# Routing of the later slots in seven operations behind the leading tokens, and six row buffers

## The chip, the cores and the metric

One core of a Trainium2 chip runs the whole computation in one launch. The metric is the device time of one execution in microseconds. TensorE (PE) multiplies matrices, VectorE (DVE) and ScalarE (ACT) do the elementwise work, GpSimd (POOL) does elementwise work and issues the gathers, SyncE (SP) issues plain transfers. Each engine has a queue of its own that it works through in order; they meet at semaphores.

## The reference, cut to what matters

Three layers follow one another. Attention of 512 tokens with 32 state rows in each of 8 x 8 heads gives 4352 tokens of 512 numbers. A mixture of 8 experts sends each token to the one expert with the highest cosine, and a dense layer with a hard-swish comes behind it:

```python
expert_idx = np.argmax(logits, axis=1)            # logits = xn @ en.T / tau
for e in range(E):
    mask = expert_idx == e
    h = np.maximum(x[mask] @ w1[e], 0.0)
    out[mask] = gate_w[mask, None] * (h @ w2[e])
h = out @ w_in
return (h * np.clip(h + 3.0, 0.0, 6.0) / 6.0) @ w_out
```

Which tokens go to which expert is known only when the attention is done. All products keep single precision: each factor is split into a high part and a low part (hi and lo, wh and wl, and so on), and three products of parts are added.

## The kernel before, in words

**Stages.** The attention runs batch by batch up to about 130 us and writes the tokens with their logits to a scratch in DRAM (xd). Tokens of one expert are packed into slots of 128 rows. The expert with the most tokens is the leading expert: its first five slots (QUAD, four slots, and FIFTH, one) are known as soon as its number and each token's rank are known, and are worked on while the routing of all other slots is still computed. Then come the later units (RUN) of two slots or one, and between them the dense layer in blocks of 256 tokens (Y loads a block's tokens, F1 and F2 are its two products). The weights of the dense layer are converted along the way (`convert`); its early parts are done beside the attention and the leading slots.

**How the order is made.** Nothing is scheduled on the chip. `Sched` is a planner that runs while the program is written: each operation is given an engine or a choice of engines with a cost in microseconds (the dict, "D" for VectorE and so on), a due time (the number behind it), operations that it waits for, and places in rings of buffers that it takes and gives back. The planner plays this through and puts next what can begin first, with 0.0473 of its due time added (0.115 before the leading slots are opened). What comes out is each engine's fixed order of instructions; the real waits are those of the semaphores. An operation is not cut: all its instructions stand together in its engine's queue.

**The routing.** `o_lead` finds the leading expert and its number (L988 to L990), `o_e0` casts the number to an integer for SP (L993), `o_s0` places the leading tokens, `o_at(0)`, `o_pg(0)` and `o_gidx(0)` turn that into row numbers for the gathers. For the later slots `o_tot` (L1017 to L1043) counts each expert's slots in small tiles, `o_slot` (L1052 to L1058) gives each token its slot, in three rounds over the first, middle and last parts of an expert's slots, then `o_at(1)`, `o_pg(1)` (L1078, 34 matmuls), `o_gidx(1)`, `o_quarter` and `o_qidx` make the row numbers; `o_es` gives SP the expert of each slot, `o_cs` the row at which each slot's output goes. On VectorE `o_es` is 5.0 us by the planner's reckoning and `o_slot` 4.2.

**Queues around the change.** SP issues the loads of expert weights (`load_w`, L1244 and L1247, four raw buffers), the stores of the five leading outputs (`out_slot`, L1551) and the loads of the dense blocks' tokens (`Y`, L1586 and L1590). It reads the expert's number with a value load (L1233) ahead of the first weights. POOL issues the gathers of tokens (`X`: L1283 whole rows, L1289 quarter rows, four to a slot) and the stores of the later slots' outputs, and does part of the low weight halves (L1261). A raw weight tile is cast on ScalarE or VectorE (wh, L1258), its rest made on VectorE or POOL (wl, L1261).

**The row buffers.** One pool of 128 x 544 buffers, `row`, NROW = 5 of them, serves gathered tokens (xg and xq), tokens of a dense block (yl), the outputs before they are stored (yt, L1543 and L1547; yo) and the middle tile of a late weight conversion (cv_m). The planner's ring `row` has as many places; a second ring, `rin`, allows four of them at a time to inputs (xg, xq, yl).

**The scratch.** `dynamic_dma_scratch_size` is the part of SBUF, in bytes of each partition, that is set aside for the descriptors of POOL's transfers.

The functions that the diff touches, with the line numbers of the profile:

Of the kernel before, what the change touches and what calls it, by code (L numbers as in the profile page):

```python
# [14 lines left out]
ALU = mybir.AluOpType  # L15
AX = mybir.AxisListType
# [22 lines left out]
class Sched:  # L39
# [16 lines left out]
    def op(self, fn, cost, prio, deps=(), take=(), give=(), dma=0.0, after=None, port=""):  # L56

        o = Op()
        o.port = port
        o.fn, o.cost, o.prio, o.take, o.give, o.dma = fn, cost, prio, take, give, dma  # L60
        o.kids, o.ready, o.end, o.left = [], -99.0, None, 0
        for h in give:
            h.readers += 1
        for d, end in [(d, True) for d in deps] + [(after, False)]:
            if d is None:
                continue
            if d.end is None:
                d.kids.append((o, end))
                o.left += 1
            else:  # L70
                o.ready = max(o.ready, d.end if end else d.issued)
        if not o.left:
            self.avail.append(o)
        self.n += 1
        return o
# [79 lines left out]
def kernel(  # L155
# [13 lines left out]
    PE, ACT, DVE, POOL, SP = nc.tensor, nc.scalar, nc.vector, nc.gpsimd, nc.sync  # L169
    PSUM, DRAM = bass.MemoryType.PSUM, bass.MemoryType.DRAM  # L170
    B, H, S, D = x.shape
# [71 lines left out]
    copy = {"A": ACT.copy, "D": DVE.tensor_copy}  # L243


    NRAW, NW, NROW, NGX = 4, 3, 5, 4
    NAX, NXT, NSC, NE2, NE1, NA2, NAH, NXR = (3, 3, 1, 1, 2, 1, 1, 1)
    NHX = 4
    RG = {n: Ring(k) for n, k in dict(
# [5 lines left out]
    def hold(*names):  # L255
        return Hold(*(RG[n] for n in names))
# [642 lines left out]
    def T(shape, name, dt=F32, home=rt):  # L899
        return home.tile(shape, dt, name=name)  # L900
# [111 lines left out]
        DVE.tensor_scalar(out, out, BIG, None, op0=ALU.add)  # L1012
        DVE.tensor_scalar(out, out, -BIG, None, op0=ALU.add)

    def o_tot():

        DVE.tensor_scalar(full, cnt, 127.0 / 256, BIG, op0=ALU.add, op1=ALU.add)  # L1017
        DVE.tensor_scalar(full, full, -BIG, None, op0=ALU.add)
        DVE.tensor_scalar(lead, key, kmax[:, 0:1], float(NL), op0=ALU.is_equal, op1=ALU.mult)
        DVE.tensor_tensor(before, key.unsqueeze(1).to_broadcast([128, E, E]),  # L1020
                          key.unsqueeze(2).to_broadcast([128, E, E]), op=ALU.is_gt)

        DVE.tensor_tensor(odd, full, lead, op=ALU.subtract)
        floor_half(npair, odd)

        def prior(out, t):
            w = T([128, E, E], "prior")
            DVE.tensor_tensor(w, before, t.unsqueeze(1).to_broadcast([128, E, E]), op=ALU.mult)
            DVE.reduce_sum(out, w, axis=AX.X)

        prior(pb, npair)
        DVE.tensor_scalar(pb, pb, float(NP), 2.0, op0=ALU.min, op1=ALU.mult)
        DVE.tensor_scalar(two, pb, -1.0, 2.0 * NP, op0=ALU.mult, op1=ALU.add)
        DVE.scalar_tensor_tensor(two, npair, 2.0, two, op0=ALU.mult, op1=ALU.min)
        DVE.tensor_tensor(single, odd, two, op=ALU.subtract)
        prior(sb, single)
        DVE.tensor_scalar(pb, pb, float(NL), None, op0=ALU.add)
        DVE.tensor_scalar(sb, sb, float(NL + 2 * NP), None, op0=ALU.add)

        DVE.tensor_tensor(lo_, pb, lead, op=ALU.subtract)  # L1040
        DVE.tensor_tensor(mid_, two, lead, op=ALU.add)
        DVE.tensor_tensor(hi_, sb, mid_, op=ALU.subtract)
        DVE.tensor_tensor(hi_, hi_, lo_, op=ALU.subtract)  # L1043

    ofs = [T([128, NTILE], f"ofs{i}") for i in range(3)]

    def o_slot():
        for i, v in enumerate((lo_, mid_, hi_)):
            for c, (j0, j1) in enumerate(PART):
                n = j1 - j0  # L1050
                t = tmp[c][:, :, 0:n]
                DVE.tensor_tensor(t, hot[c][:, :, 1:n + 1], v.unsqueeze(2).to_broadcast([128, E, n]), op=ALU.mult)  # L1052
                DVE.reduce_sum(ofs[i][:, j0:j1], t.rearrange("p e j -> p j e"), axis=AX.X)
        DVE.tensor_scalar(loc, loc, -BIG, None, op0=ALU.add)
        DVE.tensor_tensor(ofs[1], loc, ofs[1], op=ALU.is_ge)
        DVE.tensor_tensor(ofs[1], ofs[1], ofs[2], op=ALU.mult)
        DVE.tensor_tensor(ofs[0], ofs[0], ofs[1], op=ALU.add)
        DVE.tensor_tensor(s16[1], loc, ofs[0], op=ALU.add)  # L1058
# [4 lines left out]
    def o_at(i):  # L1063

        n = SLOTS[i]
        t = V["at", i] = T([128, 4 if i else 3, n, NTILE], f"at{i}", BF16)
        eq = t[:, 2]
        DVE.tensor_tensor(eq, s16[i].unsqueeze(1).to_broadcast([128, n, NTILE]), iota_sj[:, 0:n], op=ALU.is_equal)
        DVE.tensor_scalar(t[:, 0], eq, pf[:, 0:1], None, op0=ALU.mult)
        for k, v in ((1, iota_j), (3, obf[:, 0]), (2, obf[:, 1]))[:3 if i else 1]:  # L1070
            DVE.tensor_tensor(t[:, k], eq, v.unsqueeze(1).to_broadcast([128, n, NTILE]), op=ALU.mult)

    def o_pg(i):
        n, k = SLOTS[i], 4 if i else 2
        p = pool["g_ps"].tile([128, 512], F32, tag="g", name="pg_g") if i else ps("pg_ps")[:, 0, :]
        p = V["pg", i] = p[:, 0:k * n].rearrange("p (a s) -> p a s", a=k)
        for j in range(NTILE):
            PE.matmul(p, V["bt", j], V["at", i][:, 0:k, :, j], start=j == 0, stop=j == NTILE - 1)  # L1078
# [80 lines left out]
        seq_ = [b_]  # L1159
    pr = t_end - 30  # L1160
    s0_op = op(o_s0, {"D": 0.35}, pr - 1, [lead_e, *loc_])
    e0_op = op(o_e0, {"D": 0.1}, pr + 3, [lead_e])
    gidx_op = []
    for i, n in enumerate(SLOTS):
        if i:
            pr = 107.5892 + 27.0094
            tot = op(o_tot, {"D": 3.4}, pr, [lead_e, cnt_op, switched])
            slot = op(o_slot, {"D": 4.2}, pr, [tot, s0_op])
        hpg = hold("gps" if i else "ps")
        a = op(lambda i=i: o_at(i), {"D": 3.9 if i else 0.7}, pr - 1, [slot if i else s0_op])  # L1170
        b = op(lambda i=i: o_pg(i), {"T": 2.3 if i else 1.3}, pr - 1, [a, *bt_], [hpg])
        gidx_op.append(op(lambda i=i: o_gidx(i), {"D": 0.6 if i else 0.35}, pr - 2, [b], (), [hpg]))
    hpg = hold("gps")
    a = op(o_quarter, {"T": 0.3}, pr, [gidx_op[1]], [hpg])
    qidx_op = op(o_qidx, {"D": 0.7}, pr, [a], (), [hpg])
    es_op = op(o_es, {"D": 5.0}, pr, [tot])
    cs_op = op(o_cs, {"D": 1.9}, pr + 10, [es_op])
    first.append(gidx_op[0])
    first.extend([lead_e, cnt_op, s0_op, e0_op, *bt_])
    lead_ops.extend([qidx_op, cs_op])  # L1180

# [573 lines left out]

    for u in (QUAD, *RUN):  # L1760
        for w in "ab":
            for i in range(4):
                load_w(u.w, w, i, [w_at[u, w, 2 * i + j] for j in range(2)])

    for u in (QUAD, FIFTH):
        for i in range(u.n):
            X(u, i, x_at[u, i])
    for k in range(8):
        for hf in range(2):
            L1w(QUAD, k, w_at[QUAD, "a", k] + 1.28 * hf, hf)  # L1770
# [113 lines left out]
```

## Time and profile before

Three runs took 1407.59, 1408.51 and 1410.87 us, a median of 1408.51. The profiled execution took 1408.27 us, of which its span is 1406.5 us, at a mean granted TensorE clock of 0.968.

| engine | busy us | share of the span |
|---|---|---|
| PE | 1325.9 | 94% |
| PE weight loads | 1176.0 | 84% |
| DVE | 875.6 | 62% |
| ACT | 595.7 | 42% |
| POOL | 406.8 | 29% |

Shares are means over stages with different limits. The page's forty slices (35 us each) show that TensorE's busy tenths are 9 from the tenth slice on up to the last but one, and 5 to 8 before. An answer about waits puts idle time of an engine down to what came last of all that it waited for; a timeline gives it in brackets behind the instruction that it stood before.

### The profile page before, as it was taken

How to read it: one execution, taken by the hardware profiler on the slowest of the kernel's cores; microseconds unless marked ns; L12 is line 12 of the kernel's file. 1: busy time of each engine (PE TensorE's matmuls, PEld its weight loads, DVE VectorE, ACT ScalarE, POOL GpSimd, SP SyncE). 2: the span in 40 equal slices, each digit the busy share in tenths (PEclk: the TensorE clock that was granted, in tenths of full speed). 3: DMA queues.
4: the chain of work that ended last, by engine and by line, in shares of the span. 5: the costliest groups of instructions: out<-in, count | busy, mean ns of one | idle time of the engine just before them, and what ended most of it. 6: DMA issues, size and time to landing. Idle time of an engine off the chain costs nothing. (4 is left out here: it accounts for less than half of the span.)

```text
span 1406.5 us, 25411 instructions
## 1 busy us (share of the span) xinstructions
PE 1325.9 (94%) x9176; PEld 1176.0 (84%) x9176; DVE 875.6 (62%) x2069; ACT 595.7 (42%) x1296; POOL 406.8 (29%) x430
## 2 busy tenths in 40 slices
PE   7885798889999999999999999999999999999997
PEld 5664777777788989898989989898988999899996
DVE  5777865888866455565656456776767777344432
ACT  3785634676433334342434333333434343333332
POOL 3332546322533323233223223232332320100000
PEclk8996799999999999999999999999999999999999
DMA  6654446567653333343434324555554543101000
GB/s 169 180 181 152 157 128 186 182 192 228 181 177 99 107 105 116 98 117 93 124 92 111 110 85 146 162 144 159 151 166 151 166 143 128 42 14 31 16 16 15
DMA packets 151827, 176.47 MB, mean 125 GB/s; under 512 B 43856, under 2 KB 116560, under 8 KB 150672
## 3 DMA queue, kind: packets, MB, share of 16 engines
q1 hardware_dynamic: 128608, 121.47, 28.9%
q0 software_dynamic: 12336, 36.55, 8.4%
q10 hardware_dynamic: 10752, 16.78, 3.7%
q8 instruction: 73, 1.20, 0.4%
q14 instruction: 58, 0.48, 0.1%
HBM read 146.65 MB, written 28.10 MB: 124 GB/s over the span
## 5 line engine op out<-in xcount | busy, mean ns | idle before, releaser
L1629 PE MATMUL u_ps<-yh,wih 128*128 128x256 f32 x1088 | 306.4, 282 | 7.9 <-ACT yh L1605 4.9
L1629 PE MATMUL u_ps<-yw,wih 128*128 128x256 f32 x1088 | 306.5, 282 | 0.1
L1629 PE MATMUL u_ps<-yh,wil 128*128 128x256 f32 x1088 | 305.9, 281 | 0.0
L1633 ACT ACTIVATE r<-u_ps,three 128x256 f32<-128x256 f32 x272 | 129.3, 475 | 371.8 <-PE u_ps L1629 353.7
L1636 DVE SCALAR_TENSOR_TENSOR u_ps<-r,u_ps 128x256 f32<-128x256 f32 x272 | 116.5, 428 | 226.0 <-ACT r L1633 212.7
L1629 PEld LDWEIGHTS u_ps<-yh,wih 128*128 128x128 f32 x1088 | 206.5, 190 | 17.5 <-ACT yh L1605 5.1
L1664 PE MATMUL o<-woh,gh 128*128 128x512 f32 x544 | 216.5, 398 | 1.1 <-ACT yo L1680 0.9
L1664 PE MATMUL o<-wol,gh 128*128 128x512 f32 x544 | 215.7, 396 | 0.0
L1664 PE MATMUL o<-woh,gl 128*128 128x512 f32 x544 | 214.4, 394 | 0.8 <-DVE gl L1643 0.8
L1629 PEld LDWEIGHTS u_ps<-yw,wih 128*128 128x128 f32 x1088 | 205.8, 189 | 8.4 <-DVE yw L1608 0.4
L1629 PEld LDWEIGHTS u_ps<-yh,wil 128*128 128x128 f32 x1088 | 206.5, 190 | 0.0
L1261 DVE TENSOR_TENSOR wl<-raw,wh 128x512 fp32r<-128x512 f32 x278 | 193.6, 705 | 9.4 <-issue 2.4
L1640 ACT CAST gh<-u_ps 128x256 fp32r<-128x256 f32 x272 | 101.4, 373 | 202.4 <-PE o L1664 165.9
L1643 DVE TENSOR_TENSOR gl<-u_ps,gh 128x256 fp32r<-128x256 f32 x272 | 114.9, 423 | 113.3 <-ACT gh L1640 108.3
L1523 PE MATMUL y_ps<-wh,hx 128*128 128x512 f32 x512 | 184.4, 397 | 0.0
L1261 POOL TENSOR_TENSOR wl<-raw,wh 128x512 fp32r<-128x512 f32 x74 | 101.4, 1372 | 219.8 <-DVE wh L1258 90.6
L1289 POOL DMA_INDIRECT xq<-xd,qidx x128 | 130.6, 1020 | 55.1 <-issue 34.6
L1420 PE MATMUL h_ps<-xt,wh 128*128 128x256 f32 x704 | 137.2, 284 | 0.0
L1683 POOL DMA_INDIRECT out_dram<-yo,ix x34 | 38.0, 1117 | 333.6 <-DVE yo L1678 227.7
L1258 DVE CAST wh<-raw 128x512 fp32r<-128x512 f32 x245 | 106.9, 437 | 44.2 <-PE y_ps L1523 21.9
L1664 PEld LDWEIGHTS o<-woh,gl 128*128 128x128 f32 x544 | 102.1, 188 | 26.1 <-DVE gl L1643 1.2
L1664 PEld LDWEIGHTS o<-woh,gh 128*128 128x128 f32 x544 | 102.2, 188 | 18.2 <-ACT yo L1680 1.7
(297 smaller groups left out, 2204.4 us busy)
## 6 DMA issues: line engine op xcount, KB each, us to landing
raw<-in_moe_w_dram SPq DMA_DIRECT2D x176, 512.0 KB
xd<-xr SPq DMA_DIRECT2D x8, 1088.0 KB
yl<-ysd SPq DMA_DIRECT2D x136, 64.0 KB
ysd<-yt POOLq DMA_DIRECT2D x32, 256.5 KB
xb<-in_x_dram SPq DMA_DIRECT2D x48, 128.0 KB
yw<-in_moe_w_out_dram ACTq DMA_DIRECT2D x9, 512.0 KB
cv_raw<-in_moe_w_in_dram ACTq DMA_DIRECT2D x8, 512.0 KB
yh<-in_moe_w_in_dram ACTq DMA_DIRECT2D x8, 512.0 KB
```

Of the source, the lines that this page charges most:

```text
L1258: copy[e](pc["hi"], box["t"][:, j, :])
L1261: eng[e].tensor_tensor(pc["lo"], box["t"][:, j, :], f32(pc["hi"]), op=ALU.subtract)
L1289: POOL.indirect_dma_start(q[:, j * QW:(j + 1) * QW], None, xd_q, index(qidx[:, j, s:s + 1]))
L1420: PE.matmul(out(f), pc[w][:, (2 * c + f) * 128:(2 * c + f + 1) * 128], u.xt[a][:, 2 * j + c, 256 * hf:256 * hf + 256], start=new and c == ...
L1523: PE.matmul(u.y[i], u.ht[t][:, a, lo + 128 * i:lo + 128 * i + 128], pc[w], start=c == 0 and k == 0, stop=c == KF - 1 and k == 2)
L1629: PE.matmul(p, w, y[:, k, :], start=k == 0 and j == 0, stop=k == KD - 1 and j == 2)
L1633: ACT.activation(q["r"], q["p"], AF.Relu, bias=pool["three"][:, 0:1], scale=unit_i)
L1636: DVE.scalar_tensor_tensor(q["p"], q["r"], 6.0, q["p"], op0=ALU.min, op1=ALU.mult)
L1640: ACT.copy(q["h"], q["p"])
L1643: DVE.tensor_tensor(q["l"], q["p"], f32(q["h"]), op=ALU.subtract)
L1664: PE.matmul(o["o"][a], g[:, a * 128:(a + 1) * 128], w, start=m == 0 and j == 0, stop=m == KFF - 1 and j == 2)
L1683: POOL.indirect_dma_start(out, bass.IndirectOffsetOnAxis(ap=o["ix"][:, a:a + 1], axis=0), box["t"], None)
```

## The change

`o_tot` is cut into three operations and `o_slot` into four (three rounds `o_ofs`, and the rest), each with its own cost. The rounds now wait for the low parts of all five leading token tiles. The operations of the later routing are made after those of QUAD's and FIFTH's tokens and before the weight loads of `load_w`. The cast `o_e0` is due 6 us sooner. There are six row buffers rather than five; the descriptor scratch has 4096 bytes of a partition rather than 8192.

```diff
-    NRAW, NW, NROW, NGX = 4, 3, 5, 4
+    NRAW, NW, NROW, NGX = 4, 3, 6, 4
...
-    def o_tot():
+    def o_tot0():
...
         floor_half(npair, odd)
...
+    def o_tot1():
         prior(pb, npair)
...
         DVE.tensor_tensor(single, odd, two, op=ALU.subtract)
+
+    def o_tot2():
         prior(sb, single)
...
+    def o_ofs(i):
+
+        for c, (j0, j1) in enumerate(PART):
+            n = j1 - j0
+            t = tmp[c][:, :, 0:n]
+            v = (lo_, mid_, hi_)[i]
+            DVE.tensor_tensor(t, hot[c][:, :, 1:n + 1], v.unsqueeze(2).to_broadcast([128, E, n]), op=ALU.mult)
+            DVE.reduce_sum(ofs[i][:, j0:j1], t.rearrange("p e j -> p j e"), axis=AX.X)
+
     def o_slot():
-        for i, v in enumerate((lo_, mid_, hi_)):
-            for c, (j0, j1) in enumerate(PART):
...
-    e0_op = op(o_e0, {"D": 0.1}, pr + 3, [lead_e])
+    e0_op = op(o_e0, {"D": 0.1}, pr - 3, [lead_e])
     gidx_op = []
-    for i, n in enumerate(SLOTS):
+    s0_at = pr
+
+    def route(i, deps, pr):
+
         if i:
-            pr = 107.5892 + 27.0094
-            tot = op(o_tot, {"D": 3.4}, pr, [lead_e, cnt_op, switched])
-            slot = op(o_slot, {"D": 4.2}, pr, [tot, s0_op])
+            tot = op(o_tot0, {"D": 2.0}, pr, [lead_e, cnt_op, switched])
+            tot = op(o_tot1, {"D": 1.3}, pr, [tot])
+            tot = op(o_tot2, {"D": 1.5}, pr, [tot])
+            ofs_ = [op(lambda k=k: o_ofs(k), {"D": 2.1}, pr, [tot, *deps]) for k in range(3)]
+            slot = op(o_slot, {"D": 1.0}, pr, [*ofs_, s0_op])
         hpg = hold("gps" if i else "ps")
...
+        e = op(o_es, {"D": 5.0}, pr, [tot])
+        c = op(o_cs, {"D": 1.9}, pr + 10, [e])
+        lead_ops.extend([q, c])
+        return q, e, c
+
+    route(0, (), s0_at)
...
+    for u in (QUAD, FIFTH):
+        for i in range(u.n):
+            X(u, i, x_at[u, i])
+    qidx_op, es_op, cs_op = route(1, [*QUAD.x, *FIFTH.x], 107.5892 + 27.0094)
     for u in (QUAD, *RUN):
         for w in "ab":
             for i in range(4):
                 load_w(u.w, w, i, [w_at[u, w, 2 * i + j] for j in range(2)])
 
-    for u in (QUAD, FIFTH):
-        for i in range(u.n):
-            X(u, i, x_at[u, i])
...
-                    dynamic_dma_scratch_size=8192)
+                    dynamic_dma_scratch_size=4096)
```

## Rows read from the trace of the kernel before

**Rows 1.** windows over whole core: busy us per engine (count), PE clock, DMA share, GB/s

```profile
300.00:400.00 100.00, 91.10 (x536) 78.04 (x535) 86.65 (x188) 58.30 (x122) 35.69 (x35) 0.97 0.66 202
...
400.00:800.00 400.00, 399.73 (x2564) 360.69 (x2563) 223.32 (x532) 144.64 (x343) 123.45 (x126) 1.00 0.36 108
```

**Rows 2.** waits of PE, 138 to 300: us in total, times, longest

```profile
PE m_g L1314 <- issue: 9.0, 1, 9.0
...
PE h_ps L1420 <- DVE wl L1261: 6.4, 2, 4.1
...
PE u_ps L1629 <- ACT yh L1605: 4.9, 1, 4.9
```

**Rows 3.** timeline of DVE, 133 to 150: start, duration, work [idle before <-releaser]

```profile
133.41 0.08 DVE L990 DVE_READ_ACCUMULATOR e0t<-key,kmax,iota_e 128x1 f32 x1
...
136.14 0.13 DVE L993 CAST scalars<-e 1x1 int32<-1x1 f32 x1
...
141.31 1.90 DVE L1017 TENSOR_SCALAR full<-cnt 128x8 f32<-128x8 f32 x1
...
149.32 0.69 DVE L1320 TENSOR_TENSOR x<-m_g,x 128x512 fp32r<-128x512 f32 x1
```

**Rows 4.** waits of SP's queue, 125 to 260

```profile
SPq L1233 <- DVE scalars L993: 6.3, 1, 6.3
```

**Rows 5.** timeline of SP's queue, 137 to 246 (transfers issued)

```profile
137.44 2.29 SPq L1244 DMA_DIRECT2D raw<-in_moe_w_dram  x4
...
237.48 9.04 SPq L1590 DMA_DIRECT2D yl<-ysd  x8
```

**Rows 6.** windows of 1 us around the leading expert's loads

```profile
136.00:137.00 1.00, 0.80 (x13) 0.80 (x14) 0.27 (x3) 0.00 (x0) 0.00 (x0) 0.50 0.00 0
...
139.00:140.00 1.00, 0.00 (x0) 0.00 (x0) 0.96 (x2) 0.00 (x0) 0.81 (x1) 0.50 0.99 335
```

**Rows 7.** timeline of POOL, the first gather of leading tokens

```profile
139.19 1.40 POOL L1283 DMA_INDIRECT xg<-xd,gidx  x1 [12.30 <-DVE three L1199]
```

**Rows 8.** timeline of ACT, first leading token and two output copies

```profile
146.77 0.62 ACT L1309 COPY xp<-xg 128x512 f32<-128x512 f32 x1 [3.72 <-DMA xg<-xd,gidx]
...
226.71 0.69 ACT L1543 ACTIVATE yt<-y_g,gates 128x512 f32<-128x512 f32 x1
...
230.25 0.69 ACT L1543 ACTIVATE yt<-y_g,gates 128x512 f32<-128x512 f32 x1 [2.84 <-DMA ysd<-yt]
```

**Rows 9.** timeline of DVE, 157 to 236

```profile
157.50 0.69 DVE L1320 TENSOR_TENSOR xs<-m_g,xs 128x512 fp32r<-128x512 f32 x1 [0.41 <-ACT xs L1317]
...
164.69 1.36 DVE L1052 TENSOR_TENSOR tmp<-hot,lo__187 128x200 f32<-128x200 bf16 x1
...
178.68 1.27 DVE L1443 SCALAR_TENSOR_TENSOR hx<-h_g,hx 128x512 fp32r<-128x512 f32 x2
...
218.06 1.45 DVE L1341 TENSOR_TENSOR xt<-xq,xt 128x256 fp32r<-128x256 f32 x4
...
235.69 0.14 DVE L1547 COPY yt<-oidx 128x1 int32<-128x1 int32 x1
```

**Rows 10.** timeline of PE, 179 to 251

```profile
179.40 0.38 PE L1420 MATMUL h_g<-x,wh 128*128 128x256 f32 x1 [1.39 <-DVE hx L1443]
...
184.51 10.13 PE L1078 MATMUL pg_g<-at,bts 128*128 128x164 bf16 x34 [0.20 <-DVE at L1071]
...
227.27 0.28 PE L1420 MATMUL h_ps<-xt,wh 128*128 128x256 f32 x1
...
235.82 0.58 PE L1420 MATMUL h_ps<-xt,wl 128*128 128x256 f32 x1 [4.06 <-DVE wl L1261]
...
250.26 0.58 PE L1629 MATMUL u_ps<-yh,wih 128*128 128x256 f32 x1 [4.91 <-ACT yh L1605]
```

**Rows 11.** window of the stretch behind the wait of 4.06 us

```profile
235.80:241.00 5.20, 5.18 (x24) 5.18 (x25) 2.19 (x8) 0.60 (x1) 1.28 (x1) 0.50 0.64 162
```

**Rows 12.** costliest groups of the page: busy, mean ns | idle before, releaser

```profile
L1289 POOL DMA_INDIRECT xq<-xd,qidx x128 | 130.6, 1020 | 55.1 <-issue 34.6
```

More of the change, by code (lines that the diff above doesn't have):

```diff
@@ L1024, in o_tot, with prior @@
         floor_half(npair, odd)
[L1026 to L1029, printed above, removed]
+    def prior(out, t):
+        w = T([128, E, E], "prior")
+        DVE.tensor_tensor(w, before, t.unsqueeze(1).to_broadcast([128, E, E]), op=ALU.mult)
+        DVE.reduce_sum(out, w, axis=AX.X)
+    def o_tot1():
         prior(pb, npair)
@@ L1045 @@
     ofs = [T([128, NTILE], f"ofs{i}") for i in range(3)]
-    def o_slot():
-        for i, v in enumerate((lo_, mid_, hi_)):
-            for c, (j0, j1) in enumerate(PART):
[L1050 to L1053, printed above, removed]
+    def o_ofs(i):
[5 more added lines that the diff above has]
+            DVE.reduce_sum(ofs[i][:, j0:j1], t.rearrange("p e j -> p j e"), axis=AX.X)
+    def o_slot():
         DVE.tensor_scalar(loc, loc, -BIG, None, op0=ALU.add)
@@ L1161 @@
     s0_op = op(o_s0, {"D": 0.35}, pr - 1, [lead_e, *loc_])
-    e0_op = op(o_e0, {"D": 0.1}, pr + 3, [lead_e])
+    e0_op = op(o_e0, {"D": 0.1}, pr - 3, [lead_e])
     gidx_op = []
-    for i, n in enumerate(SLOTS):
+    s0_at = pr
+    def route(i, deps, pr):
         if i:
-            pr = 107.5892 + 27.0094
-            tot = op(o_tot, {"D": 3.4}, pr, [lead_e, cnt_op, switched])
-            slot = op(o_slot, {"D": 4.2}, pr, [tot, s0_op])
-        hpg = hold("gps" if i else "ps")
[L1170 to L1177, printed above, removed]
+            tot = op(o_tot0, {"D": 2.0}, pr, [lead_e, cnt_op, switched])
[3 more added lines that the diff above has]
+            slot = op(o_slot, {"D": 1.0}, pr, [*ofs_, s0_op])
+        hpg = hold("gps" if i else "ps")
+        a = op(lambda: o_at(i), {"D": 3.9 if i else 0.7}, pr - 1, [slot if i else s0_op])
+        b = op(lambda: o_pg(i), {"T": 2.3 if i else 1.3}, pr - 1, [a, *bt_], [hpg])
+        gidx_op.append(op(lambda: o_gidx(i), {"D": 0.6 if i else 0.35}, pr - 2, [b], (), [hpg]))
+        if not i:
+            return
+        hpg = hold("gps")
+        a = op(o_quarter, {"T": 0.3}, pr, [gidx_op[1]], [hpg])
+        q = op(o_qidx, {"D": 0.7}, pr, [a], (), [hpg])
+        e = op(o_es, {"D": 5.0}, pr, [tot])
[3 more added lines that the diff above has]
+    route(0, (), s0_at)
     first.append(gidx_op[0])
     first.extend([lead_e, cnt_op, s0_op, e0_op, *bt_])
-    lead_ops.extend([qidx_op, cs_op])
     mctx = ctx.enter_context(ExitStack())
```

## The prediction, made before the kernel was run

> **What bounds the kernel now.** The page first: its forty slices show TensorE at 9 tenths from the tenth slice to the last, and lower before. The windows say it sharper: TensorE is busy 399.73 of 400 us between 400 and 800, but 91.10 of 100 between 300 and 400 [rows 1]. So from 400 us on every microsecond won earlier is kept, as nothing there waits for anything but TensorE, and what the change can win lies before 400. I then asked what TensorE waited for between 138 and 300 us: 9.0 us ahead of the first transposes of the leading tokens (m_g), 6.4 us for low weight halves (wl) in two waits, 4.9 us for the first dense block's tokens (yh) [rows 2]. Those are the three waits whose queues the change touches. For each I read the timeline of the engine named, back to what held it up.
>
> The profiled execution took 1408.27 us (span 1406.5), 0.24 below the median of the three runs, 1408.51. The sum is made from 1408.27; the difference is a tenth of the 0.2% (2.8 us) that a measurement of this kernel can tell from no change.
>
> **Part 1, the number of the leading expert.** SP loads that expert's weights, and reads its number first. The number is known to VectorE at 133.49 (133.41 + 0.08), but its cast to an integer, L993, ran at 136.14 as the last of its group [rows 3]; SP waited 6.3 us for it [rows 4] and issued the four loads from 137.44 on [rows 5]. In the meantime nothing moved: 0 GB/s at 136 to 137, against 335 at 139 to 140 [rows 6]. With the due time 6 us lower the cast comes straight behind the number, so the loads can move up by 136.14 - 133.49 = 2.65 us. The gathers of the leading tokens share the transfers' time with them: the first was issued at 139.19 [rows 7], yet ScalarE could use it only at 146.77 [rows 8]. If the weights are out of the way 2.65 us sooner, the tokens land up to that much sooner. But VectorE is nearly as late: its block of totals (o_tot) starts at 141.31 and the first token's low part at 149.32 had no idle time before it [rows 3], so a sooner token finds VectorE busy unless the three pieces of o_tot let it in. Bounds: 0 and 2.65; I take the middle, **1.3 us**. The 0.13 us of the cast now stands ahead of the row numbers; it is within that.
>
> **Part 2, the routing in seven operations behind the tokens.** No instruction is added or removed: o_tot and o_slot run the same ones, in pieces. The new wait, for the low parts of all five leading tiles, is nearly met already: the last of them starts at 157.50, and o_slot began at 164.69 [rows 9]. What the cut can win is the order: o_slot and o_es ran as two blocks from 164.69 to 178.68, and the first thing behind them was a relu's low half (hx) [rows 9] for which TensorE waited 1.39 us [rows 10]. A piece of o_slot lets hx in, o_es is still one block. Bounds 0 and 1.39, taken **0.7 us**. The planner now reckons 2.0 + 1.3 + 1.5 + 3 x 2.1 + 1.0 = 12.1 us where it reckoned 3.4 + 4.2 = 7.6, so the matmuls of L1078, which took 10.13 us from 184.51 [rows 10], may be put up to 4.5 us later in TensorE's order. Behind them are the row numbers, POOL's gathers and the tokens of the first later unit, ready at 219.51 (218.06 + 1.45) [rows 9]; TensorE takes them up at 227.27 [rows 10]. That is a cover of 7.8 us, so 4.5 cost nothing and 3.3 remain. POOL has the same gathers to issue, SP the same loads.
>
> **Part 3, six row buffers.** At the end of the leading slots five stores need a row buffer each, and gathered tokens hold up to four (the ring rin). The third output copy ran at 226.71; the fourth, on ScalarE, began at 230.25 after 2.84 us of idle, released by the store of an earlier one [rows 8]. ScalarE's queue is in order, so the casts of weights behind it waited too, then VectorE's wl, then TensorE, which took up L1420 at 235.82 after 4.06 us [rows 10] and then ran slow: 5.18 us busy in 235.8 to 241 at 0.50, the 1.2 GHz level [rows 11], of which half, 2.6, is loss. The same chain holds the second wait: the fifth copy's index was written at 235.69 [rows 9], SP's loads of the dense block began at 237.48, after the fifth store [rows 5], and TensorE's first dense matmul at 250.26 came after 4.91 us [rows 10]. With a sixth buffer and still four for inputs, the fourth copy need not wait; then the fifth is the next late one, as it needs the first store landed, at 230.25. So the chain gets shorter by about one copy's wait, not by all. Bounds: on the good side 4.06 + 2.6 + 4.91 = 11.6 us; on the bad side -2.1, if the buffer goes to a conversion instead (cv_m shares this ring) and its three VectorE operations, each of the size of the 0.69 us one at 149.32 [rows 3], come ahead of wl. I take the 2.84 us of ScalarE's idle and half of the cold loss: 2.8 + 1.3 = **4.1 us**.
>
> **Part 4, the smaller scratch.** POOL issued 128 gathers of quarter rows at 1020 ns each; the idle time before them was 55.1 us in all, most of it "issue" [rows 12]. None of it is put down to a transfer, so I cost the smaller scratch at nothing; what it costs if that is wrong stands below. By the Trainium skill (DMA: Bandwidth & Descriptors, SWDGE vs HWDGE vs iDMA) descriptors of GpSimd's transfers are appended to rings that lie in a part of SBUF set aside, so half the bytes is half the descriptors in flight. That speaks against the change; no row here shows a full ring, and the sum by that rule alone would be the last rival's.
>
> **The sum:** 1.3 + 0.7 + 4.1 = 6.1 us, all before 400 us, so 1408.27 - 6.1 = 1402.2 us.
>
> **The rivals.**
> - *Both waits go altogether* (10%). The good ends: 2.65 + 1.39 + 11.6 = 15.6 us, so 1392.6. For it: the stores, the weights and the dense block's tokens hang on one ring. Against: the fifth copy still has the first store ahead of it.
> - *Handed back* (15%). Between 300 and 400 VectorE is busy 86.65 of 100 [rows 1], so the conversions of the dense weights may set the pace up to 400; TensorE then comes sooner and waits there for what part 3 gave. Left are 2.0 us: 1406.3. Against: the stalls of part 3 left VectorE idle too, and it starts its work sooner as well.
> - *The sixth buffer doesn't reach the stores* (10%). A conversion takes it in the planner's order and the fourth copy waits as before: again 1406.3. For it: the ring is one, only the inputs are limited.
> - *The later routing comes too late* (15%), the one on the other side. Seven operations with a due time of 134.6 stand behind everything more urgent; each boundary can let weight splits and relus in. If the tokens of the first later unit come 16 us later, 7.8 are covered, 8.2 are waited, and the cold stretch (2.6) comes again: 8.2 + 2.6 - 6.1 = 4.7 us slower, 1413.0. It decides from 7.8 + 6.1 - 2.6 = 11.3 us of delay. Against: six boundaries with two operations of 0.69 us each are 8.3, which is about the cover alone.
> - *The scratch binds* (5%). If each of the eight gathers for the first later unit waited one more of its own 1.02 us, that is 8.2 us against the cover of 7.8: some 0.4 us there, but the same 1.02 on all 128 is 130 us of POOL's time, most of it hidden behind TensorE. I put it at 1402 to 1412, taken as 1410.
>
> **How the numbers follow.** The forecast has 45% and its own range 1397 to 1405. Faster than before by over 0.2%, that is under 1405.7: the forecast's 45, the first rival's 10, and 8 of the 25 at 1406.3, whose time lies at the edge: 63%. Within 0.2%: the other 17. Slower: 15 + 5 = 20%. The range that should hold it 8 times in 10 reaches from just under the first rival's time to short of the fourth's: 1392 to 1411.
>
> **What the profile after would show.** L993 next to L990 and SP's four loads some 2.65 us earlier: part 1; ScalarE's first copy of a token clearly before 146.77 would show that it counted. Pieces of L1052 and L1053 with L1443 between them: part 2. No idle time of ScalarE on a store between the third and the fourth copy, wl sooner, the two waits of 4.1 and 4.9 us smaller: part 3. Transfers named in POOL's waits ahead of gathers: the scratch. The prediction is wrong if the stretch before 400 us holds as much of TensorE's idle time as before (8.9 us in 300 to 400, 4.1 and 4.9 in 230 to 250), wherever it now lies, or if a new wait for the first later unit's tokens appears.

## The result, and the profile after

The changed kernel took 1425.81 us (median of four runs, 1424.94 to 1428.35) beside 1409.25 for the kernel before: 1.0119 times its time, 95% interval 1.0105 to 1.0133. The forecast was 1402.2, range 1392 to 1411: wrong in sign and outside the range. The profiled execution took 1428.35 (span 1426.4, 19.9 more than before).

The instructions are the same in kind and nearly in number, and from 400 us on TensorE is as busy as before. The windows of the changed kernel, columns as in [rows 1]:

```profile
260.00:300.00 40.00, 34.16 (x188) 29.71 (x187) 27.34 (x57) 20.80 (x41) 7.14 (x7) 0.91 0.60 181
300.00:400.00 100.00, 82.19 (x486) 71.83 (x485) 76.28 (x173) 59.23 (x127) 38.87 (x39) 0.91 0.59 179
400.00:800.00 400.00, 398.57 (x2539) 358.74 (x2538) 225.13 (x534) 146.06 (x348) 125.79 (x126) 1.00 0.38 114
```

The first of these windows before:

```profile
260.00:300.00 40.00, 37.62 (x229) 33.43 (x228) 33.23 (x77) 27.59 (x57) 13.14 (x14) 0.96 0.72 225
```

Between 300 and 400 us TensorE is idle 17.8 us, twice the 8.9 of [rows 1], and VectorE does 10.4 us less. Of the 19.9 us, 13.3 are idle time of TensorE (1426.4 - 1332.5 after, 1406.5 - 1325.9 before), 12.4 of them between 260 and 400 us. The other 6.6 are longer busy time on the same 9176 matmuls; the granted clock was 0.91 in the windows of 260 to 300 and 300 to 400, where it had been 0.96 and 0.97. By 260 us TensorE had begun 2050 matmuls (2043 before), by 300 us 2236 (2270), by 500 us 3348 (3462). So the change was level until 260 us, and the loss lies between 260 and 500 us, where the prediction's sum had no term.

What VectorE waited for from 220 to 500 us (us in total, times, longest; two lines of that view):

```profile
DVE cv_m L316 <- DMA ysd<-yt: 11.7, 4, 5.5
...
DVE yl L1612 <- DMA yl<-ysd: 4.9, 2, 3.2
```

The first line stood at 0.4 us, once, in the kernel before. cv_m is the middle tile of a dense weight's conversion. It takes a row buffer, and the waits say that the buffer was still being stored. Line numbers after are 16 higher than before in this part of the code. VectorE's timeline of the changed kernel around the first two of those waits:

```profile
281.95 0.15 DVE L1563 COPY yt<-oidx 128x1 int32<-128x1 int32 x1
...
284.93 0.14 DVE L1563 COPY yt<-oidx 128x1 int32<-128x1 int32 x1
290.61 0.69 DVE L316 SCALAR_TENSOR_TENSOR cv_m<-yh 128x512 int32<-128x512 int32 x1 [5.54 <-DMA ysd<-yt]
291.22 0.42 DVE L1274 CAST wh<-raw 128x512 fp32r<-128x512 f32 x1
291.56 0.68 DVE L1277 TENSOR_TENSOR wl<-raw,wh 128x512 fp32r<-128x512 f32 x1
...
297.74 0.69 DVE L316 SCALAR_TENSOR_TENSOR cv_m<-yw 128x512 int32<-128x512 int32 x1 [2.60 <-DMA ysd<-yt]
```

POOL's stores of the pair's two outputs, and what TensorE and ScalarE did meanwhile (three timelines):

```profile
284.93 0.61 POOL L1570 DMA_DIRECT2D ysd<-yt  x1 [17.39 <-issue]
291.30 0.56 POOL L1570 DMA_DIRECT2D ysd<-yt  x1 [5.76 <-DVE cv_m L316]
```

```profile
292.30 0.58 PE L1436 MATMUL h_ps<-xt,wl 128*128 128x256 f32 x1 [4.16 <-DVE wl L1277]
```

```profile
291.76 0.62 ACT L323 CAST wih<-cv_m 128x512 fp32r<-128x512 f32 x1 [5.38 <-DVE wh L1274]
```

Read in order of time: the first output is stored from 284.93. VectorE, which has nothing but its own queue to follow, comes to a cv_m that needs a buffer whose store is under way, and stands still for 5.54 us. Behind it in the queue are a cast and a low half of expert weights. TensorE takes that low half up at 292.30 after 4.16 us of idle, ScalarE has waited 5.38. The second store is issued 6.37 us after the first, and the next cv_m waits again. All this is a conversion of weights that are wanted later, standing ahead of weights that are wanted now.

### The profile page after: what moved, and what is told of

It is laid out like the page before. It is cut to its first block, busy times and chain, and to the rows that moved or that the text cites. A ratio compares the mean times of both kernels' runs of the same rounds, so it can differ in the third digit from the quotient of the medians.

```text
span 1426.4 us, 25376 instructions
## 1 busy us (share of the span) xinstructions
PE 1332.5 (93%) x9176; PEld 1182.0 (83%) x9176; DVE 872.5 (61%) x2055; ACT 599.5 (42%) x1306; POOL 412.3 (29%) x434
## 5 line engine op out<-in xcount | busy, mean ns | idle before, releaser
L1277 DVE TENSOR_TENSOR wl<-raw,wh 128x512 fp32r<-128x512 f32 x273 | 188.5, 698 | 10.5 <-ACT wh L1274 4.5
L1277 POOL TENSOR_TENSOR wl<-raw,wh 128x512 fp32r<-128x512 f32 x79 | 109.1, 1382 | 265.0 <-DVE wh L1274 109.5
L1305 POOL DMA_INDIRECT xq<-xd,qidx x128 | 130.5, 1020 | 58.2 <-issue 34.0
L1436 PE MATMUL h_ps<-xt,wh 128*128 128x256 f32 x704 | 140.9, 287 | 0.0
L1436 PE MATMUL h_ps<-xt,wl 128*128 128x256 f32 x352 | 102.2, 290 | 18.5 <-DVE wl L1277 14.0
```

Source lines behind the costliest of these rows:

```text
L1277: eng[e].tensor_tensor(pc["lo"], box["t"][:, j, :], f32(pc["hi"]), op=ALU.subtract)
L1305: POOL.indirect_dma_start(q[:, j * QW:(j + 1) * QW], None, xd_q, index(qidx[:, j, s:s + 1]))
L1436: PE.matmul(out(f), pc[w][:, (2 * c + f) * 128:(2 * c + f + 1) * 128], u.xt[a][:, 2 * j + c, 256 * hf:256 * hf + 256], start=new and c == ...
```

## The experiments

All runs stand beside runs of the kernel before on the same chip (medians 1408.97 to 1409.99). The last three columns are read from the traces: waits of VectorE's cv_m for a store in 240 to 500 us, waits of TensorE for weight halves (wl, wh) of the other engines in 240 to 400 us, and the matmuls begun by 500 us. They come from the one execution that was profiled, which can lie at the edge of the range: 1404.97 us in e3, 1425.72 in e13. "Plan" is the number of row buffers that the planner counts; "memory" is how many there are.

| kernel | plan / memory | scratch | us, median (range) | ratio, 95% interval | cv_m | wl, wh | by 500 |
|---|---|---|---|---|---|---|---|
| before | 5 / 5 | 8192 | 1409.25 (1407.59 to 1410.87) | 1 | 0.4 | 8.0 | 3462 |
| changed | 6 / 6 | 4096 | 1425.81 (1424.94 to 1428.35) | 1.0119 [1.0105, 1.0133] | 11.7 | 23.1 | 3348 |
| e1_rows | 6 / 6 | 4096 | 1411.06 (1407.84 to 1413.90) | 1.0021 [1.0011, 1.0030] | 4.0 | 10.5 | 3489 |
| e2_routing | 5 / 5 | 8192 | 1411.17 (1410.17 to 1413.36) | 1.0018 [1.0008, 1.0028] | 1.0 | 14.2 | 3419 |
| e3_scratch | 5 / 5 | 4096 | 1412.85 (1404.97 to 1416.05) | 1.0044 [1.0028, 1.0059] | 0.9 | 8.5 | 3474 |
| e4_e0 | 5 / 5 | 8192 | 1412.74 (1410.64 to 1416.13) | 1.0027 [1.0014, 1.0040] | 0.3 | 15.6 | 3441 |
| e9_row5_scr4096 | 5 / 5 | 4096 | 1410.05 (1406.51 to 1414.27) | 1.0009 [0.9996, 1.0022] | 0.9 | 14.1 | 3442 |
| e5_ring5 | 5 / 6 | 4096 | 1409.29 (1406.15 to 1415.27) | 0.9998 [0.9981, 1.0014] | 2.6 | 15.1 | 3432 |
| e10_scr_big | 6 / 6 | 7680 | 1422.30 (1421.59 to 1425.16) | 1.0096 [1.0079, 1.0112] | 11.7 | 20.7 | 3356 |
| e6_cvm_own | 5 + 1 / 5 + 1 | 4096 | 1412.68 (1410.15 to 1416.21) | 1.0023 [1.0011, 1.0035] | 0 | 12.2 | 3399 |
| e11_cvm_same_order | 6 / 5 + 2 | 4096 | 1454.31 (1453.52 to 1455.61) | 1.0321 [1.0299, 1.0342] | 0 | 18.5 | 3356 |
| e7_store_time | 6 / 6 | 4096 | 1411.86 (1407.80 to 1415.65) | 1.0017 [1.0001, 1.0033] | 8.4 | 8.1 | 3422 |
| e8_e0_back | 6 / 6 | 4096 | 1418.37 (1414.63 to 1421.09) | 1.0066 [1.0048, 1.0084] | 6.1 | 8.4 | 3402 |
| e12_before_pool6 | 5 / 6 | 7680 | 1412.44 (1409.34 to 1414.87) | 1.0022 [1.0006, 1.0038] | 3.0 | 10.6 | 3463 |
| e13_six_and_two | 6 / 6 + 2 | 3584 | 1420.48 (1418.03 to 1425.72) | 1.0061 [1.0037, 1.0085] | 0 | 17.9 | 3350 |
| e14_six_and_two_planned | 6 + 2 / 6 + 2 | 3584 | 1414.49 (1409.56 to 1418.90) | 1.0028 [1.0009, 1.0047] | 0 | 13.7 | 3414 |
| e15_scr3584 | 6 / 6 | 3584 | 1422.02 (1419.18 to 1424.29) | 1.0083 [1.0070, 1.0097] | 11.9 | 18.0 | 3365 |
| e16_six_and_two_again | 6 / 6 + 2 | 3584 | 1409.80 (1405.39 to 1414.21) | 1.0003 [0.9990, 1.0015] | 0 | 12.7 | 3470 |
| e17_six_and_two_third | 6 / 6 + 2 | 3584 | 1418.52 (1416.56 to 1422.80) | 1.0064 [1.0048, 1.0080] | 0 | 17.7 | 3397 |
| e18_change_again | 6 / 6 | 4096 | 1429.32 (1427.89 to 1430.74) | 1.0137 [1.0121, 1.0154] | 11.4 | 20.0 | 3320 |

**The parts one at a time.** e1 is the kernel before with

```diff
-    NRAW, NW, NROW, NGX = 4, 3, 5, 4
+    NRAW, NW, NROW, NGX = 4, 3, 6, 4
...
-                    dynamic_dma_scratch_size=8192)
+                    dynamic_dma_scratch_size=4096)
```

> The kernel before with six row buffers and the scratch of 4096, and the routing as it was. Theory R (rows): with a sixth buffer the planner lets a conversion's middle tile (cv_m) take a buffer whose output store is still under way; VectorE's queue stands still for it (11.7 us in 260 to 400 in the changed kernel), so this alone gives nearly the whole loss, 1421 to 1428 us. Theory O (order of the routing): the seven operations with their larger costs shift the order of everything behind; then this alone is at 1405 to 1411. Theory S (scratch): slower here and in the scratch-only run alike.

e2 is the changed kernel with those two lines as before, so the routing and e0 alone.

> The changed kernel with five row buffers and the scratch of 8192, so the routing and the cast's due time alone. Theory R: 1403 to 1411, no VectorE wait of more than 3 us for a store ahead of cv_m. Theory O: 1421 to 1428, TensorE idle in 280 to 400 as in the changed kernel (about 18 us). Theory S: 1403 to 1411.

e3 is the kernel before with the scratch line alone, e4 the kernel before with e0's due time alone:

```diff
-    e0_op = op(o_e0, {"D": 0.1}, pr + 3, [lead_e])
+    e0_op = op(o_e0, {"D": 0.1}, pr - 3, [lead_e])
```

> The kernel before with the scratch of 4096 and nothing else. Theories R and O: every engine's order is that of before, 1407 to 1411. Theory S: 1418 or more, and waits of GpSimd ahead of gathers that the kernel before does not have.

> The kernel before with the cast of the leading expert's number due 6 us sooner and nothing else. The prediction's part 1: 0 to 2.65 us faster by 150 us, 1406 to 1408 if the order behind stays as good. Theory R and theory O leave this open; if the mere reshuffling of the order costs much (theory P: any edit of due times throws the planner's order about), it is off by 5 us or more in either direction.

No part costs more than 3.9 us alone, and none gains. Rows with the smaller scratch (e1) and routing alone (e2) add up to some 4 us; together they cost 16.6. The loss is an interaction, which none of the theories had as it came.

**Order, buffers or scratch.** The planner writes a fixed order for every engine; it changes with what it is told, not with what memory holds. With five row buffers in the plan, e9 and e5 have e2's order instruction for instruction; e10 has the changed kernel's. e9 is the changed kernel with NROW back at 5; the others:

```diff
 e5:
-... row=NROW, rin=4,
+... row=5, rin=4,
 e10:
-                    dynamic_dma_scratch_size=4096)
+                    dynamic_dma_scratch_size=7680)
 e6 (NROW 5; cvm=1 added to the rings, a pool "cvm" of one tile added):
-... hold(*("cv",) if early else ("row", "cvl"))
+... hold(*("cv",) if early else ("cvm",))
-pool["row"].tile([128, W], F32, tag="row", name="cv_m")[:, 0:512]
+pool["cvm"].tile([128, 512], F32, tag="cvm", name="cv_m")
```

> The changed kernel with five row buffers, in the pool and in the planner, and the small scratch of 4096: the instruction order of every engine is that of e2_routing (1411.2 us with the scratch of 8192), so that only the scratch differs. The whole change costs 16.6 us (1425.8 against 1409.25). Theory R (the loss is in the order that the planner writes for six row buffers, in which VectorE's cv_m stands behind a store under way): 1411 to 1415, e2 plus nothing up to the 3.9 us that e3_scratch cost alone. Theory S (the small scratch is the loss, and it is dearer once the routing is moved): 1420 to 1426.

> The changed kernel with six row buffers in the pool, but the planner counting five: the order of every engine is that of e2_routing and e9_row5_scr4096, only each row buffer is taken again one tile later. Theory R (it is the order): no dearer than e9, 1407 to 1415, and the waits of VectorE's cv_m for ysd<-yt smaller than e9's. Theory B (the sixth buffer itself is the loss: it lets transfers start earlier that collide): over e9 by 5 us or more, 1417 to 1426. Theory S: like e9, 1420 to 1426.

> The changed kernel with the scratch of the dynamic DMAs at 7680 rather than 4096, the most that fits beside six row buffers: the order of every engine is that of the changed kernel. Theory R: 1421 to 1427, the changed kernel less at most the 3.9 us of e3_scratch. Theory S: 1408 to 1414, most of the 16.6 us is back.

> The changed kernel with five row buffers for outputs and loads, and the sixth buffer's room given to the conversions alone (one 128x512 tile of their own for cv_m, in the pool and in the planner): VectorE's cv_m can wait for no store. Theory R: cv_m <-DMA ysd<-yt, 11.7 us over 260 to 420 us in the changed kernel, goes to 0, and most of the loss with it: 1408 to 1415. Theory P (any order that differs from the one before loses by chance, since the conversions land among other work): 1411 to 1426, with other waits in cv_m's place. Theory S: 1420 or more, since the scratch is 4096 here as well.

Six buffers in memory with the other order are as good as five (e5, 1409.29, though its cv_m waited 2.6 us where less than e9's 0.9 was expected); the changed kernel's order with nearly all of the scratch still loses 13 us (e10). So neither the buffer nor the scratch loses the time by itself: it takes the order that six in the plan give. Where conversions are off the row buffers, most of the loss is gone as well (e6), but under another order, which proves less.

**What in the order.** e11 was to keep the order and take cv_m's wait away, by a change in memory alone, under the plan of six. e7 and e8 change the plan; e12 gives the kernel before a sixth buffer in memory (NROW 6, the ring row=5, the scratch 7680).

```diff
 e11 (and cv_m from pool["cvm"], as in e6):
-... ("row", dict(bufs=NROW)), ("woa" ...
+... ("row", dict(bufs=5)), ("cvm", dict(bufs=2)), ("woa" ...
 e7:
-              (), [hy], dma=0.73, after=...
+              (), [hy], dma=0.73 if u.lead else 3.0, after=...
 e8:
-    e0_op = op(o_e0, {"D": 0.1}, pr - 3, [lead_e])
+    e0_op = op(o_e0, {"D": 0.1}, pr + 3, [lead_e])
```

> The changed kernel with the order of every engine kept as it is (the planner still counts six row buffers with the conversions among them), but in memory the row tiles have five buffers and cv_m two of its own: no cv_m can stand for a store. e10_scr_big had that order and lost 13 us, e6_cvm_own had another order and no such waits and lost 3.5. Theory R1 (VectorE's waits of cv_m for ysd<-yt, 11.7 us at 285 to 300 and later, and what stands behind them in the queues, are the loss): 1408 to 1415. Theory R2 (the rest of that order is the loss: POOL idle 17.4 us ahead of a store at 284.9, the weights' low parts behind it; the waits only fill time that is lost anyway): 1418 to 1427. Between, both.

> The changed kernel with the planner told that a store of a row buffer by POOL takes 3.0 us of the DMA rather than 0.73, nearer to the 5.6 us from issue to landing of the store that VectorE waited for at 285 to 290.6: its order differs from there on. Theory R1: the planner places cv_m later or elsewhere, the waits of cv_m for ysd<-yt fall below 5 us and the time to 1410 to 1419. Theory R2: 1418 to 1427. Theory P (any reordering moves the time by chance): anywhere from 1409 to 1427 whatever the waits of cv_m do.

> The changed kernel with the due time of e0 put back, 6 us later. Its order differs from the changed kernel's from the leading slots on. Theory R1 with the ring of six as sufficient cause: cv_m waits for ysd<-yt of 8 us or more again and 1419 to 1427. Theory P: the bad place is an accident of one order, so this one need not have it: cv_m waits under 5 us and 1408 to 1415.

> The kernel before with six row buffers in memory, the planner counting five, and the scratch at 7680: the order of every engine is that of the kernel before, so that only the waits for a buffer's store can go. The prediction's step on the sixth buffer (4.1 us gained where the stores' waits go, 11.6 at the most): 1398 to 1406. If those waits are hidden behind the cold clock and the loads: 1407 to 1411. Theory S (any smaller scratch costs): 1411 to 1414.

e11 missed its question: its order counts on six row buffers for outputs and loads at times and had five, and the wait went over to the output copies. Its waits of VectorE and of ScalarE in 220 to 500 us:

```profile
DVE yt L1563 <- DMA ysd<-yt: 25.4, 7, 5.6
```

```profile
ACT yt L1559 <- DMA ysd<-yt: 22.6, 6, 4.6
```

These 48 us stand beside 45 us lost, but they are not its price. By 500 us e11's TensorE had begun 3356 matmuls, the changed kernel's 3348; what makes e11 slower than the changed kernel comes later. Windows of e11 and then of the changed kernel, and the longest of e11's waits of TensorE between 500 and 800:

```profile
500.00:800.00 300.00, 282.68 (x1767) 254.23 (x1766) 150.29 (x369) 100.43 (x242) 85.95 (x84) 0.96 0.32 97
500.00:800.00 300.00, 298.82 (x1910) 269.18 (x1909) 168.15 (x400) 108.80 (x260) 93.80 (x93) 1.00 0.35 107
```

```profile
PE o L1680 <- ACT yo L1696: 12.7, 4, 6.9
```

yo is an output of the dense layer, and it takes a row buffer too. So e11 shows what one row buffer fewer costs under this order, and says nothing on cv_m.

e7 came out at 1411.86, in R1's range, but with 8.4 us of cv_m waits left where R1 wanted under 5, and TensorE's waits for weights at 8.1 us, the level of before. So a wait of cv_m need not cost its length: it seems to cost where a wanted weight stands behind it. e8 lost half (8.8 us) with half the waits (6.1), but its waits for weights are at the level of before too (8.4), so this reading does not explain it and its loss stays open. e12 shows what part 3 had been about: with the order of before, a sixth buffer gains nothing. Its 1412.44 lies where the smaller scratch was expected to put it, which e12 cannot tell apart.

e13 puts right what e11 had wrong: six row buffers beside the two tiles, at a scratch of 3584. e14 tells the planner of it as well.

```diff
 e13, e16 and e17 (and cv_m from pool["cvm"], as in e6):
-... ("row", dict(bufs=NROW)), ("woa" ...
+... ("row", dict(bufs=NROW)), ("cvm", dict(bufs=2)), ("woa" ...
-                    dynamic_dma_scratch_size=4096)
+                    dynamic_dma_scratch_size=3584)
 e14, besides (and cvm=2 added to the rings):
-... hold(*("cv",) if early else ("row", "cvl"))
+... hold(*("cv",) if early else ("cvm",))
```

> The changed kernel with the order of every engine kept as it is, six row buffers as in it, and cv_m in two buffers of its own beside them (the scratch at 3584 to make room): what e11 meant to do without its loss of a row buffer, which brought 48 us of waits of yt for ysd<-yt on VectorE and ScalarE in the place of cv_m's. Theory R1 (cv_m's waits for a store are the loss): those waits 0 and 1408 to 1415. Theory R2 (the rest of that order is the loss): waits 0 and 1418 to 1427.

> As e13, but the planner knows of it: six row buffers for loads and outputs, two for cv_m alone, so that its order may use them. R1: 1403 to 1412, since no conversion waits for a store and outputs have a buffer more than before. R2, or if the buffers never were the limit: 1409 to 1415, as e6.

e13 spoke for R2: no cv_m wait, and still 1420.48. e14, at 1414.49, came no nearer to the kernel before than e6. But e13's scratch differed from the changed kernel's, so the pair was run side by side: e15 is the changed kernel with the scratch line of e13 alone, e16 is e13's kernel again; then e17, the same a third time, beside e18, the changed kernel itself.

> The changed kernel with the scratch at 3584, the one that e13 had, and nothing else: the order of every engine is the changed kernel's, cv_m in the row buffers. What e13_six_and_two differs from it by is then cv_m's waits for a store alone. Theory R1 holds for a part: this 1424 to 1429, and 4 to 9 us above e16, the kernel of e13 in the same runs. Theory R2 alone: within 2 us of e16.

> The kernel of e13_six_and_two once more, in the same runs as e15_scr3584: same order, same scratch, same six row buffers, and no wait of cv_m for a store. R1 for a part: 1417 to 1422. R2 alone: within 2 us of e15.

> The kernel of e13_six_and_two and e16_six_and_two_again a third time. The two gave 1420.5 (on one chip) and 1409.8 (on another). Theory R1 (the waits of cv_m for a store are the whole loss, and e13 was disturbed ahead of the stretch, where TensorE had started 40 matmuls fewer by 260 us than in e16): 1408 to 1413. Theory R2 (part of the loss is in the rest of the order): 1416 to 1422.

> The changed kernel itself, in the same runs as e17. By R1 1422 to 1428 and 10 us or more above e17; by R2 4 to 6 us above it.

Side by side, with the order of every engine the same, taking cv_m off the row buffers gives 12.2 us (1422.02 - 1409.80) on one chip and 10.8 us (1429.32 - 1418.52) on another; the intervals don't touch. In the second pair the scratch differs as well (4096 in e18, 3584 in e17). Neither theory had it all: 12.2 us are more than the 4 to 9 of R1 for a part, and e17 itself lies in R2's range.

The edit does a second thing: loads and outputs have the six buffers to themselves. A wait of SP for a row buffer ahead of a block's tokens, 10.6 us in e15, is gone in e16; the weight loads behind it are issued 8.8 us later in e15 (326.40 and 317.60), no more than VectorE's lag there. When the time is lost can be read from the cv_m's themselves, which come in one order in all four traces (VectorE's timelines, start in us; the waits of e15 are 5.33, 2.72, 1.52 and 2.31 us, those of e18 5.54, 2.70, 1.10 and 2.06):

| cv_m | e16 | e15 | later by | e17 | e18 | later by |
|---|---|---|---|---|---|---|
| last before the first wait | 275.59 | 279.22 | 3.63 | 279.55 | 281.04 | 1.49 |
| at the second wait | 288.48 | 298.59 | 10.11 | 292.94 | 301.33 | 8.39 |
| last before the third wait | 329.35 | 338.50 | 9.15 | 334.06 | 340.78 | 6.72 |
| at the fourth wait | 340.36 | 353.01 | 12.65 | 344.77 | 354.83 | 10.06 |

Over the first two waits the lag grows by 6.5 us in e15 and 6.9 in e18, over the last two by 3.5 and 3.3, and between them it does not grow: 10.0 and 10.2 us at the waits. The trace of e16 in the stretch shown above, VectorE, then POOL:

```profile
283.06 0.15 DVE L1563 COPY yt<-oidx 128x1 int32<-128x1 int32 x1
283.12 0.68 DVE L316 SCALAR_TENSOR_TENSOR cv_m<-yh 128x512 int32<-128x512 int32 x1
283.72 0.42 DVE L1274 CAST wh<-raw 128x512 fp32r<-128x512 f32 x1
284.06 0.69 DVE L1277 TENSOR_TENSOR wl<-raw,wh 128x512 fp32r<-128x512 f32 x1
...
288.48 0.69 DVE L316 SCALAR_TENSOR_TENSOR cv_m<-yw 128x512 int32<-128x512 int32 x1
```

```profile
280.98 0.61 POOL L1570 DMA_DIRECT2D ysd<-yt  x1 [21.28 <-ACT r L1649]
284.81 0.56 POOL L1570 DMA_DIRECT2D ysd<-yt  x1 [3.22 <-DVE wl L1277]
```

The same cv_m follows the same index copy at once, the low half behind it starts at 284.06 rather than 291.56, and TensorE is back at the level of before between 300 and 400:

```profile
300.00:400.00 100.00, 90.20 (x540) 78.31 (x541) 83.24 (x180) 57.19 (x124) 39.19 (x39) 0.96 0.68 205
```

What e16's kernel keeps over the kernel before is not settled: 0 us in e16, 9.4 in e17, 10.7 in e13, the same program, while the kernel before was at 1409 to 1410 beside each. In e13 and e17 TensorE waited 17.9 and 17.7 us for weight halves (12.7 in e16). In e13 it was 40 matmuls behind e16 by 260 us (2015 against 2055), ahead of the stretch; in e17 it was not (2054), and lost 73 by 500 us (3397 against 3470).

The traces show where. Taken in order, e17's matmuls begin 0.2 us later than e16's at 260 us of e16, 4.0 at 270, 4.4 at 360 and 10.3 at 369. Both steps stand behind an operation of ScalarE (r) that reads a product of TensorE. In e16 it begins 0.04 us after the last matmul of the product (361.27 + 0.28), in e17 3.40 us after it (365.69 + 0.28), and TensorE then waits for a weight half. ScalarE in e16, in e17, and TensorE in e17:

```profile
361.59 0.48 ACT L1649 ACTIVATE r<-u_ps,three 128x256 f32<-128x256 f32 x1 [2.17 <-PE u_ps L1645]
```

```profile
369.37 0.47 ACT L1649 ACTIVATE r<-u_ps,three 128x256 f32<-128x256 f32 x1 [5.54 <-PE y_ps L1539]
```

```profile
372.69 0.80 PE L1539 MATMUL y_ps<-wh,hx 128*128 128x512 f32 x1 [2.53 <-DVE wh L1274]
```

The earlier step has the same beginning, at 260.98 in e17 beside 256.79 in e16. e13 has both steps (3.9 and 6.0 us); at the operation shown ScalarE begins 3.49 us after the product in e13, 4.84 in e18 and 3.29 in the first trace of the changed kernel. What held ScalarE is not shown. VectorE's idle time for which a trace names no releaser tells the executions apart: 0.2 us in e15 and in e16, 25.9 in e17, 31.5 in e18, 32.8 in e13, and 24.0 and 21.2 in the first traces of the changed kernel and the one before. It is no trait of the chip, for e1 to e4 ran on e13's chip with 0.2 to 3.0 us. Read so, the changed order costs 12.0 us where nothing begins late (e15), all of it with cv_m's waits, and 20.25 where it does (e18), 10.8 of it with them. That the late beginnings are the rest was not tried.

No version beat the kernel before; e5, e9 and e16 came level with it.

## Why the prediction was wrong

**The failed step is part 3**, and in it the bound on the bad side. It named the case, a sixth buffer that goes to a conversion (cv_m shares this ring), with its operations ahead of wl, and priced it at 2.1 us: three operations of VectorE at 0.69. What stands ahead of wl is not VectorE's work but its wait: 5.54 us for the store of the buffer, then 2.60 and two more, 11.7 in all, and in the pairs 10.8 and 12.2 us of the time. The term was mis-sized more than five times over, because it took a wait at the head of an in-order queue as if the buffer were free. The rival built on it (a conversion takes it, 1406.3, 10%) had the right mechanism and the wrong sign. The prediction looked for it at the end of the leading slots, at 220 to 240 us; it came at 285 and later, at the pairs' outputs.

Why the planner writes such an order can be read from its figures. It puts a store by POOL down at 0.73 us of transfer and some 2 us of latency, and takes the two of a pair as running together. In the trace the second is issued 6.37 us after the first in the changed kernel (3.83 in e16), and in the kernel before 5.1 to 6.3 us, for its first three pairs (POOL's timeline):

```profile
279.33 0.61 POOL L1554 DMA_DIRECT2D ysd<-yt  x1 [8.07 <-ACT yt L1543]
285.62 0.56 POOL L1554 DMA_DIRECT2D ysd<-yt  x1 [5.68 <-ACT yt L1543]
331.58 0.60 POOL L1554 DMA_DIRECT2D ysd<-yt  x1 [14.07 <-ACT yt L1543]
337.15 0.56 POOL L1554 DMA_DIRECT2D ysd<-yt  x1 [4.97 <-ACT gh L1640]
373.52 0.61 POOL L1554 DMA_DIRECT2D ysd<-yt  x1
378.57 0.56 POOL L1554 DMA_DIRECT2D ysd<-yt  x1 [4.44 <-ACT gh L1640]
```

What ties the second store to the first was not tried; the releasers named there are what ended last by time. By the planner's figures the buffers come free 3.6 us (1.04 + 0.64 + 0.73 + 1.2) and 4.7 us (1.04 more) from the start of the first issue; the changed kernel's cv_m had them after 5.7 (290.61 - 284.93) and 12.8 (297.74 - 284.93). With five in the plan that rarely met a cv_m (waits of 0.3 to 1.0 us where memory held five too); with six it did in each order (4.0 to 11.9), and e7, told 3.0 instead of 0.73, lost only 2.3 us. That the planner's figure is the root is an argument that e7 fits; e7 moved the order as well.

**The good side of part 3** gave next to nothing. Three copies of outputs now run together, but the fourth still waits for a store, and the wait went over to VectorE, which came to that copy's index and stood 3.45 us (timelines of ScalarE and VectorE, changed kernel, beside the last two lines of [rows 8]):

```profile
226.44 2.09 ACT L1559 ACTIVATE yt<-y_g,gates 128x512 f32<-128x512 f32 x3 [0.72 <-PE y_g L1539]
...
231.71 0.69 ACT L1559 ACTIVATE yt<-y_g,gates 128x512 f32<-128x512 f32 x1 [1.23 <-DMA ysd<-yt]
```

```profile
231.69 0.15 DVE L1563 COPY yt<-oidx 128x1 int32<-128x1 int32 x1 [3.45 <-DMA ysd<-yt]
```

TensorE's two waits there, 4.06 and 4.91 us in [rows 10], became:

```profile
236.56 0.58 PE L1436 MATMUL h_ps<-xt,wl 128*128 128x256 f32 x1 [4.45 <-DVE gates L1384]
249.88 0.53 PE L1645 MATMUL u_ps<-yh,wih 128*128 128x256 f32 x1 [3.28 <-ACT yh L1621]
```

The first is still a wait for wl: VectorE's wl starts at 235.83 and ends at 236.50, just ahead. So of 4.1 us taken, 1.2 came (4.06 + 4.91 - 4.45 - 3.28).

**Part 1** happened and gave nearly nothing. SP's loads moved from 137.44 to 134.54, 2.90 us against 2.65 predicted; TensorE's wait for the first tokens went from 9.0 [rows 2] to 8.7 us:

```profile
134.54 2.90 SPq L1260 DMA_DIRECT2D raw<-in_moe_w_dram  x4
```

```profile
PE m_g L1330 <- DVE l L1364: 8.7, 1, 8.7
```

The bottom bound, 0, was nearly the value; the middle was a choice without a row. Alone, the cast's due time (e4) cost 3.8 us. **Part 2**: relus' low halves do run between the pieces of the offsets (161.84 and 168.97) and the 1.39 us wait is gone; the routing's matmuls begin 3.74 us later than in [rows 10], at 188.25, within the 4.5 foreseen, but wait 2.8 us for VectorE there. The tokens of the first later unit are ready at 224.41 (222.62 + 1.79), 4.9 later than in [rows 9]. The cover of 7.8 us held: no wait for those tokens appeared, and e2, the routing and e0 alone, lost 2.2 us rather than gaining 2.0.

```profile
188.25 10.18 PE L1084 MATMUL pg_g<-at,bts 128*128 128x164 bf16 x34 [2.80 <-DVE at L1077]
```

**Part 4** stands as far as rows tell: the gathers took 1020 ns each as in [rows 12], with 58.2 us of idle before them (55.1), none put down to a transfer. The smaller scratch cost 3.9 us in e3, whose runs lie 11 us apart, nothing against e2 in e9 (1410.05 and 1411.17), and 3.5 us between e10 and the changed kernel, neither of these pairs side by side; at 3584 the changed kernel was no dearer than at 4096 (e15, 1422.02). The Trainium skill (DMA: Bandwidth & Descriptors, SWDGE vs HWDGE vs iDMA) has such descriptors appended to rings in a part of SBUF. No run here shows a ring full, nor a time that follows the size of the scratch.

**The rivals.** Handing back named the right place, 300 to 400 us, but could only take back a gain. The later routing had the right sign by a mechanism that didn't come. The 20% for slower were too few: the change rewrites the order of every engine, and each part alone lost 2 to 4 us of which the sum had no term. The page's slices were read loosely at the outset: the last of the forty is at 7 tenths, not 9, and the sixth is at 9 already; no term rests on it.

## What to carry to other kernels

Where a planner writes the order, a buffer added in a ring that several kinds of work share is a new order before it is a buffer: ask which work the planner will pull forward with it, and what a wait of that work at the head of its queue holds up. Price such a wait by the transfer that ends it, from the timeline, not by the instructions that stand in the way. And try a ring of its own for work that is wanted late, so that it can't stand behind a transfer of work that is wanted now: in the two pairs that gave back 12.2 and 10.8 us, but it needs room of its own, for with a row buffer taken away for it (e11) the kernel was slowest of all.

## What the runs showed of the hardware

Kernels with the same instructions in the same order, and other places in memory, can differ by more than the interval of a comparison. e3 differs from the kernel before by the size of a reserved area alone: 1.0044 [1.0028, 1.0059], with runs from 1404.97 to 1416.05 us. One program gave 1409.80, 1418.52 and 1420.48 us (e16, e17, e13), while the kernel before stayed within 1 us beside them. In the two slower ones, by the traces, ScalarE took up a finished product 3.40 and 3.49 us late where e16 took it up at once. So a pair side by side on one chip is worth more than two ratios that were taken apart; from e13 alone cv_m's share would have been put at a third of the loss.
